# Attention of the first batch by halves of its queries, to start the MLP's first tile earlier

## The chip, the cores and the metric

One core of one Trainium2 chip. The metric is the device time of the whole kernel in microseconds (us), median of several runs. "Ratio" always means: the mean time of one kernel's fast runs over that of the kernel before in the same rounds, so it is not quite the ratio of the medians that are quoted.

## The reference

Softmax attention over 8 batches, 12 heads, 448 positions, head size 64; then a two-layer MLP on the joined heads.

```python
scores = q @ k.T / 8;  attn = softmax(scores);  x = attn @ v      # (8, 12, 448, 64)
x = x.transpose(0, 2, 1, 3).reshape(3584, 768)
h = x @ w_in                                                        # w_in  768 x 2048
out = maximum(0.01 * h, h) @ w_out                                  # w_out 2048 x 768
```

## The kernel before

Heads are taken in pairs: 8 batches x 6 pairs = 48 units. Each unit has eight steps (`slots`). The MLP works on tiles of 384 or 512 token columns; its matmuls ("atoms") are strewn between the steps of later units, so that TensorE always has something to do while ScalarE computes exps. Tile 0 needs the first 384 queries of all six pairs of batch 0, so it cannot start before pair 5 is done. TensorE executes in program order: an MLP matmul that waits holds up the attention behind it.

```python
    def slots(u):                       # eight steps of one pair, shortened
        def s0(): scores(u, 0); scores(u, 1); expo(u, 0)
        def s1(): expo(u, 1); x_transposes(u - 2); dma_transposes(u + 2)
        def s2(): pv(u - 1, 0)
        def s3():
            load(u + 5)                                        # q, k, v of a later pair, SyncE queue
            load_w({2: 1, 3: 2, 4: 2, 5: 2}.get(u, 0))         # weights, GpSimd queue, f32 -> bf16
            transposes(u + 1)                                  # q and k, by TensorE
        def s4(): scores(u, 2); scores(u, 3); expo(u, 2)
        def s5(): expo(u, 3); cast(u + 3)                      # f32 -> bf16 on GpSimd
        def s6(): pv(u - 1, 1)
        ...
    # ... the prologue casts pairs 0 to 2 and issues the first quarter of w_in behind cast(0) ...

    def mlp(i):
        ...
        for m in range(MD):                                    # 16 blocks; a quarter of w_in holds 4
            ps = ps_mm.tile([P, 4 * P], F32, name="mm")        # two PSUM buffers
            for kk in range(KD):                               # 6
                nc.tensor.matmul(ps[:, :n], w_in_sb[:, kk, ts(m, P)], xT[:, kk, at:at + n], ...)
                if kk == KD - 1:
                    nc.scalar.activation(h[:, m, :n], ps[:, :n], AX.Prelu, alpha=0.01)
                yield n
        # ... second product with w_out, 6 results of 16 matmuls of 384 columns ...

    begin = [8 * (HP * (i + 1) + 1) + 7 - 5 * (i == 0) for i in range(B)]   # tile 0 from step 58
    # ... the atoms of tile i are spread evenly over the steps begin[i] to begin[i + 1] ...
```

The softmax here doesn't subtract the row's maximum and nothing guards it: scores larger than these inputs give would overflow.

## Time and profile before

| | before |
|---|---|
| time, median of 4 runs | 427.48 us (426.62 to 428.27) |
| first MLP matmul | 36.16 us |
| first matmul of the second MLP tile (step 111) | 84.50 us |
| span of the profiled run | 425.7 us |

The page cuts the span into 40 slices of 10.6 us; a digit is the busy share of a slice in tenths (for PEclk the granted TensorE clock, for DMA the busy share of the 16 DMA engines).

```profile
PE   6889999999999999999999999999999999999995
...
ACT  4887774467534675466643576456743477214300
...
PEclk8899999999999999999999999999999999999999
DMA  8999999995546765784464977667446450230022
```

TensorE (PE) is full from the fourth slice on. In the second and third slice ScalarE (ACT) is as busy as TensorE, and it sets the pace, as the timelines below show. DMA stays at eight to nine tenths or more for nine slices, to about 95 us: up to about 74 us because the pairs are loaded far ahead and the weights come at the same time.

The timeline of TensorE for one pair in that early stage (start us, length us, engine, line, operation, tile, shapes, count; in brackets the idle time before it and what ended it). L178 are scores, L196 the product with v, L166 and L217 transposes.

```profile
23.82 0.37 PE L217 MATMUL tr<-ident,x 112*128 112x112 bf16 x4
24.03 0.67 PE L196 MATMUL pv<-v,e 112*128 112x65 bf16 x16
24.67 0.55 PE L166 MATMUL tr<-ident,qkb 112*128 112x112 bf16 x8
25.16 0.55 PE L178 MATMUL sc<-qkT 64*128 64x448 bf16 x4
25.64 0.68 PE L196 MATMUL pv<-v,e 112*128 112x65 bf16 x16
26.59 0.36 PE L178 MATMUL sc<-qkT 64*128 64x448 bf16 x2 [0.27 <-DVE rec L203]
27.40 0.36 PE L178 MATMUL sc<-qkT 64*128 64x448 bf16 x2 [0.44 <-ACT e L187]
```

A pair repeats every 3.87 us (the next pair's x transposes start at 27.69 us). ScalarE paces this stage: its four exps of a pair take 3.34 us, with 0.54 us of idle.

```profile
21.75 3.34 ACT L187 ACTIVATE e<-sc 112x896 bf16<-112x896 f32 x4 [0.54 <-PE sc L178]
```

Which waits of TensorE there are before the second tile (waits table, up to 84.5 us: who waited for whom, us in total, times, longest):

```profile
PE sc L178 <- ACT e L187: 3.7, 9, 0.6
PE mm L134 <- DVE warm L131: 1.2, 1, 1.2
PE sc L178 <- DVE rec L203: 1.1, 4, 0.3
```

The start of the MLP and of its second tile, from the timeline of TensorE:

```profile
36.16 0.81 PE L239 MATMUL mm<-xT,w_in_sb 128*128 128x384 bf16 x4
...
84.50 1.03 PE L239 MATMUL mm<-xT,w_in_sb 128*128 128x512 bf16 x3
```

### The profile page before, as it was taken

Reading aid. Unit: us, or ns where it says so; the run is one execution under the profiler, and the core shown is the slowest. Engines: PE = TensorE matmul, PEld = TensorE weight load, DVE = VectorE, ACT = ScalarE, POOL = GpSimd, SP = SyncE. Lnnn points to the kernel's source line nnn. Section 1 sums busy time; section 2 is a strip of 40 time slices with the busy share of each in tenths; the row PEclk is TensorE's granted clock in tenths of the full one; section 3 lists DMA queues with packets and bytes.
Section 4 is the critical chain, followed back from the end, with each engine's and each line's share of the span. In section 5 each row is a group of like instructions: output and inputs, shape, how many; then the busy total and the mean of one; then the engine's idle time right before and its main releaser. Section 6 shows DMA issues by size and latency. Waiting matters only on the chain.

```text
span 425.7 us, 8968 instructions
## 1 busy us (share of the span) xinstructions
PE 411.4 (97%) x3709; PEld 226.3 (53%) x3724; DVE 100.2 (24%) x271; ACT 229.9 (54%) x322; POOL 92.1 (22%) x168
## 2 busy tenths in 40 slices
PE   6889999999999999999999999999999999999995
PEld 2555655544555555544455555554455555654562
DVE  1454323211222212311123212321123211320021
ACT  4887774467534675466643576456743477214300
POOL 5583332422111313112211131221112100000000
PEclk8899999999999999999999999999999999999999
DMA  8999999995546765784464977667446450230022
GB/s 219 257 246 245 249 249 197 256 253 118 125 117 167 209 125 158 187 209 108 104 148 131 183 180 145 177 178 170 117 99 161 99 84 18 56 85 2 0 75 74
DMA packets 98505, 63.66 MB, mean 150 GB/s; under 512 B 55456, under 2 KB 94880, under 8 KB 98464
## 3 DMA queue, kind: packets, MB, share of 16 engines
q1 hardware_dynamic: 90928, 56.56, 55.3%
q0 software_dynamic: 7296, 6.29, 9.4%
q8 instruction: 29, 0.48, 0.5%
q10 hardware_dynamic: 240, 0.23, 0.2%
q14 instruction: 12, 0.10, 0.1%
HBM read 45.61 MB, written 11.01 MB: 133 GB/s over the span
## 4 chain that ended last, share of the span: by engine, by line
PE 83%; DMA 12%; POOL 2%; ACT 1%; issue 1%; DVE 0%; SPq 0%; POOLq 0%
PE mm L256 33%; PE mm L239 31%; PE pv L196 9%; PE sc L178 9%; DMA fv<-in_v_dram 5%; DMA qkT<-qkb 4%; DMA fk<-in_k_dram 2%; DMA xT<-x 1%; ACT e L187 1%; PE tr L166 1%; POOL w_out_sb L124 1%; POOL v L111 1%; POOL w_in_sb L124 0%; POOL qkb L109 0%; POOL qkb L110 0%
## 5 line engine op out<-in xcount | busy, mean ns | idle before, releaser
L187 ACT ACTIVATE e<-sc 112x896 bf16<-112x896 f32 x192 | 167.6, 915 | 107.2 <-PE sc L178 107.2
L239 PE MATMUL mm<-xT,w_in_sb 128*128 128x384 bf16 (+1 forms) x753 | 160.3, 352 | 0.8
L256 PE MATMUL mm<-w_out_sb,h 128*128 128x384 bf16 x896 | 160.2, 326 | 0.0
L256 PEld LDWEIGHTS <-h 128*128 128x128 bf16 x896 | 81.7, 98 | 62.4 <-issue 14.1
L239 PEld LDWEIGHTS <-w_in_sb 128*128 128x128 bf16 x768 | 68.3, 97 | 70.3 <-issue 16.3
L244 ACT ACTIVATE h<-mm 128x384 bf16<-128x384 f32 (+1 forms) x128 | 69.8, 545 | 60.0 <-PE mm L239 59.9
L111 POOL CAST v<-fv 112x512 bf16<-112x512 f32 x48 | 29.6, 617 | 196.1 <-PE pv L196 163.2
L196 PEld LDWEIGHTS <-e 112*128 112x128 bf16 x1536 | 61.4, 98 | 15.6 <-DVE x L204 1.9
L203 DVE RECIPROCAL rec<-pv 112x4 f32<-112x4 f32 x96 | 17.5, 183 | 206.1 <-PE pv L196 205.3
L196 PE MATMUL pv<-v,e 112*128 112x65 bf16 x1536 | 65.3, 194 | 0.1
L178 PE MATMUL sc<-qkT 64*128 64x448 bf16 x384 | 55.4, 360 | 6.0 <-ACT e L187 3.7
L261 DVE COPY o<-mm 128x384 f32<-128x384 f32 x56 | 31.2, 557 | 90.0 <-PE mm L256 89.9
L204 DVE TENSOR_TENSOR x<-pv,rec 112x256 bf16<-112x256 f32 x96 | 40.7, 424 | 3.5 <-DVE rec L203 0.3
L109 POOL CAST qkb<-fq 112x512 bf16<-112x512 f32 x47 | 28.9, 615 | 37.4 <-DMA fq<-in_q_dram 20.6
L178 PEld LDWEIGHTS <-qkT 64*128 64x128 bf16 x384 | 12.1, 94 | 37.7 <-issue 31.3
L110 POOL CAST qkb<-fk 112x512 bf16<-112x512 f32 x47 | 28.9, 614 | 11.8 <-DMA fk<-in_k_dram 11.6
L166 PE MATMUL tr<-ident,qkb 112*128 112x112 bf16 x96 | 7.8, 226 | 1.3 <-POOL qkb L109 0.8
L169 DVE COPY qkT<-tr 128x896 bf16<-128x896 bf16 x12 | 7.4, 620 | 5.4 <-PE tr L166 5.3
L166 PEld LDWEIGHTS <-qkb 112*128 112x128 bf16 x96 | 6.2, 104 | 3.6 <-POOL qkb L109 1.3
L218 DVE COPY xT<-tr 128x448 bf16<-128x448 bf16 x9 | 3.5, 392 | 12.1 <-PE tr L217 12.1
L134 PE MATMUL mm<-warm 128*128 128x512 bf16 x8 | 3.4, 600 | 1.2 <-DVE warm L131 1.2
L124 POOL DMA_DIRECT2D w_out_sb<-in_moe_w_out_dram x4 | 3.5, 877 | 0.0
(17 smaller groups left out, 14.1 us busy)
## 6 DMA issues: line engine op xcount, KB each, us to landing
fq<-in_q_dram SPq DMA_DIRECT2D x48, 224.0 KB, 3.9
fv<-in_v_dram SPq DMA_DIRECT2D x48, 224.0 KB, 4.3
fk<-in_k_dram SPq DMA_DIRECT2D x47, 224.0 KB, 4.1
w_in_sb<-in_moe_w_in_dram POOLq DMA_DIRECT2D x4, 768.0 KB, 15.1
w_out_sb<-in_moe_w_out_dram POOLq DMA_DIRECT2D x4, 768.0 KB, 35.3
out_dram<-o SPq DMA_DIRECT2D x8, 336.0 KB, 3.1
out_dram<-o SPq DMA_DIRECT2D x8, 288.0 KB, 2.7
out_dram<-o SPq DMA_DIRECT2D x8, 240.0 KB, 3.3
```

The lines of the kernel that those rows point to most:

```text
L109: by[0](qk_sb[u][:, 0].rearrange("p so h d -> p h so d"), fq)
L110: by[1](qk_sb[u][:, 1].rearrange("p so h d -> p h so d"), fk)
L111: by[2](v_sb[u % NV][:, :, :, :D], fv)
L166: nc.tensor.transpose(tr[:, i, ts(so, SC)], qk_sb[u][:, i, so], ident[:SC, :SC])
L178: nc.tensor.matmul(ps[:, j, :S], t[j * D:(j + 1) * D, S + c * SC:S + c * SC + P], t[j * D:(j + 1) * D, :S], start=True, stop=True,)
L187: nc.scalar.activation(e[:, :, c, :], sc_t.pop((u, c))[:SC, :, :S], AX.Exp, scale=scale)
L196: nc.tensor.matmul(ps[:, qc, :], e[:, at:at + P], vt[:, j, c, :], start=(c == 0), stop=(c == NSC - 1),)
L204: nc.vector.tensor_mul(x_t[u][:, :, j, :], ps[:SC, :, :D], rec.to_broadcast([SC, NSC, D]))
L239: nc.tensor.matmul(ps[:, :n], w_in_sb[:, kk, ts(m, P)], xT[:, kk, at:at + n], start=(kk == 0), stop=(kk == KD - 1),)
L244: nc.scalar.activation(h[:, m, :n], ps[:, :n], AX.Prelu, alpha=0.01)
L256: nc.tensor.matmul(ps[:, :NW], h[:, m, ts(c, P)], w_out_sb[:, m, ts(w, NW)], start=(m == 0), stop=(m == MD - 1),)
L261: nc.vector.tensor_copy(o[c][:, ts(w, NW)], ps[:, :NW])
```

## The change

Intent: the MLP's first tile starts earlier. For batch 0 each pair is cut into two halves of 224 queries. The first halves of all six pairs run ahead of most second halves, and tile 0's first product runs in two column passes: the first pass (columns 0 to 223) needs only first halves. So it may start after 10 of 12 half-pairs (5.25 pairs' worth of exps) instead of after 7.25 pairs. The weights, loaded as before by the GpSimd queue, are moved behind the cast of pair 5, so that the pairs are not held up by them.

```diff
-    load_w()                                  # prologue, behind cast(0)
+    halves = [(0, 0), (0, 1), (1, 0), (2, 0), (1, 1), (3, 0), (4, 0), (2, 1),
+              (5, 0), (3, 1), (4, 1), (5, 1)]
+    def half_scores(h, cp): ...               # 4 matmuls of 224 columns, one exp of 896
+    def half_pv(h): ...                       # 16 matmuls, one reciprocal, two multiplies
+    def half_x_transposes(h): ...             # 2 transposes, one copy, PSUM tile "tr"
...
+        for lo, hi in ((0, SH), (SH, n)) if i == 0 else ((0, n),):    # SH = 224
+            for m in range(MD): ...           # as before, on columns lo to hi
...
+    half_casts = {1: 3, 3: 4, 5: 5, 8: 6, 10: 7}
+    half_w = {5: 4, 8: 2, 10: 2}
+    half_turns = {1: 1, 2: 2, 4: 3, 5: 4, 7: 5, 11: 6}
+    def half_slots(h):                        # four steps of a half
+        def s0(): half_scores(h, 0)
+        def s1():
+            if h in half_turns: transposes(half_turns[h])      # PSUM tile "tr" too; pool of one
+            if h >= 2: half_x_transposes(h - 2)
+        def s2(): half_scores(h, 1)
+        def s3(): half_pv(h - 1); ...loads, casts, load_w...
...
-    begin = [8 * (HP * (i + 1) + 1) + 7 - 5 * (i == 0) for i in range(B)]
+    begin = [8 * (HP * (i + 1) + 1) + 7 for i in range(B)]
+    begin[0] = 4 * (NH - 2) + 2               # step 42; step 111 stays the start of the second tile
```

More of the change, by code (lines that the diff above doesn't have):

```diff
@@ L52 @@
     r_pool = ctx.enter_context(tc.tile_pool(name="rec", bufs=4))
+    xh_pool = ctx.enter_context(tc.tile_pool(name="xh", bufs=3))
     x_pool = ctx.enter_context(tc.tile_pool(name="x", bufs=3))
@@ L73 @@
     QL = 2 * S
+    SH = S // 2
+    EH = 2 * NSC * SH
     qkT = [qk_pool.tile([P, QL + P - SC], BF16, name=f"qkT{i}") for i in range(NQ)]
@@ L140 @@
         nc.gpsimd.memset(t[:, EL:], 0.0)
+        nc.gpsimd.memset(t[:, EH:EH + P - SC], 0.0)
     for t in qkT:
@@ L218, in x_transposes, with half_scores, half_pv, half_x_transposes @@
         nc.vector.tensor_copy(dst, tr[:, 0, :])
+    halves = [(0, 0), (0, 1), (1, 0), (2, 0), (1, 1), (3, 0), (4, 0), (2, 1),
+              (5, 0), (3, 1), (4, 1), (5, 1)]
+    assert len(halves) == 2 * HP
+    xh_t = {}
+    def half_scores(h, cp):
+        u, ph = halves[h]
+        ps = ps_s.tile([P, 2, 512], F32, name="sc")
+        t = qkT[u % NQ]
+        for i in range(2):
+            c = 2 * cp + i
+            for j in range(2):
+                nc.tensor.matmul(
+                    ps[:, j, ts(i, SH)],
+                    t[j * D:(j + 1) * D, S + c * SC:S + c * SC + P],
+                    t[j * D:(j + 1) * D, ts(ph, SH)],
+                    start=True, stop=True,
+                )
+        e = e_sb[h % NE][:, :EH].rearrange("p (j c s) -> p j c s", j=2, c=NSC)
+        nc.scalar.activation(
+            e[:, :, 2 * cp:2 * cp + 2, :],
+            ps[:SC, :, :S].rearrange("p j (c s) -> p j c s", c=2), AX.Exp, scale=scale,
+        )
+    def half_pv(h):
+        u, _ = halves[h]
+        e, vt = e_sb[h % NE], v_sb[u % NV]
+        ps = ps_pv.tile([P, NSC, D + 1], F32, name="pv")
+        for j in range(2):
+            for qc in range(2):
+                for c in range(NSC):
+                    at = (j * NSC + c) * SH + qc * SC
+                    nc.tensor.matmul(
+                        ps[:, 2 * j + qc, :], e[:, at:at + P], vt[:, j, c, :],
+                        start=(c == 0), stop=(c == NSC - 1),
+                    )
+        x = xh_pool.tile([SC, 2, 2, D], BF16, name="xh")
+        rec = r_pool.tile([SC, NSC, 1], F32, name="rec")
+        nc.vector.reciprocal(rec, ps[:SC, :, D:])
+        for j in range(2):
+            nc.vector.tensor_mul(
+                x[:, :, j, :], ps[:SC, 2 * j:2 * j + 2, :D],
+                rec[:, 2 * j:2 * j + 2].to_broadcast([SC, 2, D]),
+            )
+        xh_t[h] = x
+    ready = {0: 0}
+    def half_x_transposes(h):
+        u, ph = halves[h]
+        x = xh_t.pop(h)
+        tr = ps_tr.tile([P, 2, S], BF16, name="tr")
+        for qc in range(2):
+            nc.tensor.transpose(tr[:, 0, ts(qc, SC)], x[:, qc], ident[:SC, :SC])
+        nc.vector.tensor_copy(xT[:, u, ts(ph, SH)], tr[:, 0, :SH])
+        if u == HP - 1:
+            ready[0] = (ph + 1) * SH
     def store(o, t0):
@@ L235, in mlp @@
         h = h_pool.tile([P, MD, 4 * P], BF16, name="h")
-        for m in range(MD):
-            ps = ps_mm.tile([P, 4 * P], F32, name="mm")
-            for kk in range(KD):
-                nc.tensor.matmul(
-                    ps[:, :n], w_in_sb[:, kk, ts(m, P)], xT[:, kk, at:at + n],
-                    start=(kk == 0), stop=(kk == KD - 1),
-                )
-                if kk == KD - 1:
-                    nc.scalar.activation(h[:, m, :n], ps[:, :n], AX.Prelu, alpha=0.01)
-                yield n
+        for lo, hi in ((0, SH), (SH, n)) if i == 0 else ((0, n),):
+            for m in range(MD):
+                ps = ps_mm.tile([P, 4 * P], F32, name="mm")
+                assert i or hi <= ready[0]
+                for kk in range(KD):
+                    nc.tensor.matmul(
+                        ps[:, :hi - lo], w_in_sb[:, kk, ts(m, P)], xT[:, kk, at + lo:at + hi],
+                        start=(kk == 0), stop=(kk == KD - 1),
+                    )
+                    if kk == KD - 1:
+                        nc.scalar.activation(
+                            h[:, m, lo:hi], ps[:, :hi - lo], AX.Prelu, alpha=0.01
+                        )
+                    yield hi - lo
         todo = [(c, w) for c in range(n // P) for w in range(2)]
@@ L264, in mlp, with s0, s2, s3 @@
                 yield NW
+    loads = {6: (9,), 7: (10, 11), 8: (12, 13)}
+    half_loads = {0: 5, 5: 6, 8: 7, 10: 8}
+    half_casts = {1: 3, 3: 4, 5: 5, 8: 6, 10: 7}
+    half_w = {5: 4, 8: 2, 10: 2}
+    half_turns = {1: 1, 2: 2, 4: 3, 5: 4, 7: 5, 11: 6}
+    def half_slots(h):
+        def s0():
+            half_scores(h, 0)
+        def s1():
+            if h in half_turns:
+                transposes(half_turns[h])
+            if h >= 2:
+                half_x_transposes(h - 2)
+        def s2():
+            half_scores(h, 1)
+        def s3():
+            if h >= 1:
+                half_pv(h - 1)
+            if h in half_loads:
+                load(half_loads[h])
+            if h in half_casts:
+                cast(half_casts[h])
+            load_w(half_w.get(h, 0))
+        return [s0, s1, s2, s3]
+    NH = len(halves)
     def slots(u):
@@ L279, in s1 @@
                 expo(u, 1)
-            if 2 <= u <= NU + 1:
+            if u - HP < 2:
+                half_x_transposes(NH - 2 + u - HP)
+            elif u <= NU + 1:
                 x_transposes(u - 2)
@@ L284, in s2 @@
         def s2():
-            if 1 <= u <= NU:
+            if u == HP:
+                half_pv(NH - 1)
+            elif u <= NU:
                 pv(u - 1, 0)
         def s3():
-            load(u + 5)
-            load_w({2: 1, 3: 2, 4: 2, 5: 2}.get(u, 0))
+            for i in loads.get(u, (u + 5,)):
+                load(i)
             if u + 1 < NU:
@@ L302, in s5 @@
                 expo(u, 3)
+            if u == HP:
+                cast(u + 2)
             cast(u + 3)
         def s6():
-            if 1 <= u <= NU:
+            if HP < u <= NU:
                 pv(u - 1, 1)
@@ L312, in slots @@
         return [s0, s1, s2, s3, s4, s5, s6, s7]
-    steps = [s for u in range(NU + 2) for s in slots(u)]
-    begin = [8 * (HP * (i + 1) + 1) + 7 - 5 * (i == 0) for i in range(B)]
+    steps = [s for h in range(NH) for s in half_slots(h)]
+    steps += [s for u in range(HP, NU + 2) for s in slots(u)]
+    begin = [8 * (HP * (i + 1) + 1) + 7 for i in range(B)]
+    begin[0] = 4 * (NH - 2) + 2
     assert begin[B - 1] == 8 * (NU + 1) + 7
```

## The prediction

> **What bounds the kernel now.** From about 36 us on TensorE: in the table of stretches it is busy 10.00 of every 10 us from 40 to 70, 49.8 to 49.9 of every 50 up to 400. Before 36 us it is ScalarE: four exps take 3.34 us of each 3.87 us pair (timeline), while TensorE needs about 2.6 us for a pair. The MLP, the only filler, starts at 36.2 us; some 17 us of TensorE are lost before it. DMA is full from 1 to 77 us (share 0.9 or more, 247 GB/s).
>
> **What the change does.** The MLP starts at step 42 instead of 58, after 5.25 pairs of exp rather than 7.25. Tile 0 is spread over 69 steps instead of 53. Its first product becomes 96 matmuls of 224 and 96 of 160 columns instead of 96 of 384 (0.163 us each in a run); scaled, 0.095 + 0.07 us, so +0.3 to +1 us of TensorE, and 16 more Prelus. Scores at half width: little. The intent is sound: a half costs two exps, 1.9 us, so by exp alone the MLP could start at 26.5 us, worth about 2 x 1.25 us of TensorE idle.
>
> **What eats it: the weights.** DMA packet records of the trace: pairs alone land one per 2.7 us; with both queues active a w_in quarter takes 6.35 us and a pair 5.8 us, equal bytes each (0.49 MB per 4 us). The Trainium skill, "DMA: Bandwidth & Descriptors", section "Queues, rings and completion order", says the engines round-robin between queues; the trace agrees. From issue on GpSimd to the first packet are another 5.7 us (20.05 to 25.74). Before, quarters were in at 18.5, 32.2, 38.5, 44.9 us, just ahead of the MLP. After, the first weight issue sits behind the cast of pair 5 on GpSimd: pair 5 lands about 19.2, cast until 19.9, first packet about 25.6. Loads of later pairs run ahead, so the queues stay shared. Quarters are usable at about 32.7, 39, 45.5 and 52 us. A pass-1 quarter (24 narrow matmuls, 2.3 us, plus 5 steps of attention at 0.33 us) needs only 4 us, so TensorE, in order, stalls about 6 us at 26.5 and about 2.4 us at each further quarter, attention behind it.
>
> **Sum.** Last quarter 52, plus 2.4 of matmuls and 1.7 of attention: pass 1 (step 62) ends near 56. The other 49 steps: pass 2, 7 + 4.6; second product 15.7 + 11.0: step 111 at about 94.5. Before it was reached at 84.5. From there both are the same and TensorE-bound, so the 10 us are kept, all on the critical path. w_out (7.1 us a quarter) should land at 59 to 81, just in time.
>
> **Predicted:** 437 us, range 431 to 443. Faster by over 2%: 0.03; within 2%: 0.30; slower by over 2%: 0.67.
>
> **What would show it.** First MLP matmul at 32 to 33 us, not 26, TensorE waiting there for w_in (waits table); three more such waits at quarter borders; the clock row dropping near 27 to 35; the second tile's 512-column matmuls beginning near 95 us instead of 84.5.
>
> **What would make it wrong.** Pair loads running dry of buffers while GpSimd is blocked, so quarters take about 4 us: then the stalls mostly vanish and it is 427 to 430. A first packet earlier than 5.7 us after issue: a gain of the same size. Slower: a half clock in the bursts, or DMA transposes of pair 12 late (they cost 0.5 us at 71 already).

## More of the kernel before

The lengths of neighbours overlap in the pipeline; from start to next start, as the chain of waits counts them, sixteen matmuls of `pv` take 0.51 us.

The trace's clock records say: full from 4.20 us, half from 7.61, full again from 14.44 to 424 us.

## The result

| | before | changed |
|---|---|---|
| median of 4 runs | 427.48 us | 440.44 us (439.37 to 440.98) |
| ratio | | 1.030 (95%: 1.0268 to 1.0332) |
| first MLP matmul | 36.16 us | 38.71 us |
| second column pass (step 62) | | 59.51 us |
| second MLP tile (step 111) | 84.50 us | 98.18 us |
| from there to the end | 341.2 us | 341.0 us |
| bytes of 1, 2, 3, 4 w_in quarters moved by, us | 18.5, 32.2, 38.5, 44.9 | 31.1, 37.4, 43.7, 50.1 |
| w_in quarters landed (semaphore), us | 19.2, 33.8, 40.1, 46.4 | 32.0, 38.7, 45.0, 51.6 |

The row of bytes counts all packets of the weights' queue. A quarter can be used only when its semaphore reports the landing, some 0.6 to 1.6 us later in these two traces.

The changed kernel is 3% slower, and the whole loss is made before the second tile starts: 98.18 - 84.50 = 13.7 us; what follows is the same in both. The slices of the changed kernel (11.0 us each):

```profile
PE   7889899999999999999999999999999999999995
...
ACT  4555677566654377446754377546754377304300
...
PEclk9999999999999999999999999999999999999998
DMA  9999999389565676586454677587655540130022
```

ScalarE, which paced the early stage before (8, 8, 7), now is at 5; TensorE is as busy as before. The clock row shows 9 from the start, and it must not be believed here, as the timeline of TensorE shows. L237 are half scores, L257 the product with v, L170 and L278 the transposes:

```profile
21.33 0.56 PE L237 MATMUL sc<-qkT 64*128 64x224 bf16 x4
21.82 0.93 PE L170 MATMUL tr<-ident,qkb 112*128 112x112 bf16 x8
23.47 0.35 PE L278 MATMUL tr<-ident,xh 112*128 112x112 bf16 x2 [0.71 <-DVE qkT L173]
23.75 0.55 PE L237 MATMUL sc<-qkT 64*128 64x224 bf16 x4
24.23 1.06 PE L257 MATMUL pv<-v,e 112*128 112x65 bf16 x16
25.23 0.56 PE L237 MATMUL sc<-qkT 64*128 64x224 bf16 x4
26.09 0.37 PE L278 MATMUL tr<-ident,xh 112*128 112x112 bf16 x2 [0.31 <-DVE xh L265]
```

The same 16 matmuls of `pv` that took 0.67 us in the kernel before take 1.06 us here (0.51 and 0.99 us from start to next start), the same eight transposes 0.93 us for 0.55. TensorE runs at half speed. The trace's first clock record of this run is "full from 43.78 us"; before it there is none, and the row prints 9 for what is not recorded. Two of the four runs list a mean clock of 0.997 and 0.999, the other two 0.961 and 0.958 (over 438 us that is some 34 to 37 us at half speed), and all four are equally long (440.98, 439.37, 440.27, 440.61 us): what differs is whether the slow stretch was recorded. In the trace of experiment 3, which has the same half stage, the records do say half, from 15.00 to 42.30 us (there the gate had opened twice before, from 4.76 and from 11.59 us, and each time shut again after 3.41 us).

So from 6.5 to 38.7 us the chain of waits runs through TensorE and, in each half, through one of two short steps of VectorE (DVE) that it waits for: the copy of the q and k transposes, or the multiply that makes x. The waits table (up to 98.1 us) sums them up:

```profile
PE tr L278 <- DVE qkT L173: 3.6, 5, 0.7
PE tr L278 <- DVE xh L265: 1.6, 5, 0.3
PE mm L304 <- ACT h L309: 1.2, 3, 0.6
```

There is no wait for w_in at all. A half takes 2.65 us, or 3.9 us where q and k are transposed in it, instead of the 1.9 us that two exps cost; ScalarE idles beside it:

```profile
24.40 0.92 ACT L244 ACTIVATE e<-sc 112x896 bf16<-112x896 f32 x1 [1.56 <-PE sc L237]
```

The start of the MLP, the moment at which the clock opens, and the second tile, from the timeline:

```profile
38.71 1.11 PE L304 MATMUL mm<-xT,w_in_sb 128*128 128x224 bf16 x5
...
42.06 1.11 PE L304 MATMUL mm<-xT,w_in_sb 128*128 128x224 bf16 x5
...
44.73 0.64 PE L304 MATMUL mm<-xT,w_in_sb 128*128 128x224 bf16 x5
...
98.18 1.02 PE L304 MATMUL mm<-xT,w_in_sb 128*128 128x512 bf16 x4
```

Five matmuls of 224 columns take 1.11 us up to 43 us and 0.64 us from 44.7 us on. The MLP itself opened the clock.

Why does it stay shut? The Trainium skill, "TensorE: Matmul & The Clock Gate", Part 1 ("What's actually happening"), says that half speed is the default and that a busy window of about 3.4 us opens the gate. The records agree in length: the intervals of the kernel before are 3.41 and 6.83 us. I cut both traces into windows of 3.41 us, counted from the opening, with the table of stretches. In the changed kernel TensorE was busy for 2.50 to 3.11 us of each window between 6.2 and 40.4 us, and the gate stayed shut; the first window with 3.41 us (40.37 to 43.78) opened it. In the kernel before a window with 3.21 us (11.03 to 14.44) did. Once open, it stayed open at 2.70 us. Three rows of the changed kernel's table (stretch, its length, TensorE's busy time, matmuls, then the clock, which reads 1.00 where nothing is recorded, the DMA share and GB/s):

```profile
36.96:40.37 3.41, 3.10 (x33) 1.00 1.18 247
40.37:43.78 3.41, 3.41 (x29) 1.00 1.18 245
43.78:47.20 3.42, 2.70 (x40) 1.00 1.18 245
```

And the row of the kernel before:

```profile
11.02:14.44 3.42, 3.21 (x33) 0.50 1.17 246
```

The theory, then: **the waits of 0.3 and 0.7 us in every half keep the gate shut, and at half speed TensorE paces the stage (clock theory).** The rival is the prediction's: **late weights (weights theory).** The weights arrived nearly when predicted, but the slow stage had pushed the MLP back so far that each quarter was there before it was needed. Whether they would have cost as much with an open clock has to be tried.

### The profile page after: what moved, and what is told of

It reads as the page before. It is cut to its first block, busy times and chain, and to the rows that moved or that the text cites. A ratio compares the mean times of both kernels' runs of the same rounds, so it can differ in the third digit from the quotient of the medians.

```text
span 439.2 us, 9300 instructions
## 1 busy us (share of the span) xinstructions
PE 425.1 (97%) x3868; PEld 239.4 (55%) x3868; DVE 102.6 (23%) x289; ACT 233.5 (53%) x338; POOL 92.1 (21%) x171
## 4 chain that ended last, share of the span: by engine, by line
PE 94%; ACT 2%; DVE 2%; DMA 1%; issue 0%; ACTq 0%
PE mm L323 34%; PE mm L304 34%; PE pv L200 10%; PE sc L182 9%; PE pv L257 2%; PE sc L237 2%; PE tr L170 2%; ACT e L191 1%; DVE qkT L173 1%; DMA fk<-in_k_dram 1%; PE tr L278 1%; DVE xh L265 1%; ACT h L309 0%; DVE rec L263 0%; ACT e L244 0%
## 5 line engine op out<-in xcount | busy, mean ns | idle before, releaser
L191 ACT ACTIVATE e<-sc 112x896 bf16<-112x896 f32 x168 | 148.1, 915 | 99.3 <-PE sc L182 98.7
L304 PE MATMUL mm<-xT,w_in_sb 128*128 128x512 bf16 (+3 forms) x864 | 166.0, 335 | 1.4 <-ACT h L309 1.2
L304 PEld LDWEIGHTS <-w_in_sb 128*128 128x128 bf16 x864 | 75.8, 98 | 70.4 <-issue 19.3
L309 ACT ACTIVATE h<-mm 128x512 bf16<-128x512 f32 (+3 forms) x144 | 72.4, 504 | 62.3 <-PE mm L304 62.3
L200 PEld LDWEIGHTS <-e 112*128 112x128 bf16 x1344 | 54.1, 98 | 12.1
L200 PE MATMUL pv<-v,e 112*128 112x65 bf16 x1344 | 56.8, 194 | 0.0
L182 PE MATMUL sc<-qkT 64*128 64x448 bf16 x336 | 46.4, 355 | 0.0
L208 DVE TENSOR_TENSOR x<-pv,rec 112x256 bf16<-112x256 f32 x84 | 35.7, 425 | 2.9
L244 ACT ACTIVATE e<-sc 112x896 bf16<-112x896 f32 x24 | 21.9, 917 | 15.6 <-PE sc L237 15.6
L182 PEld LDWEIGHTS <-qkT 64*128 64x128 bf16 x336 | 9.6, 94 | 27.3 <-issue 23.7
L237 PE MATMUL sc<-qkT 64*128 64x224 bf16 x96 | 13.0, 374 | 1.4 <-DVE qkT L173 0.7
L257 PEld LDWEIGHTS <-e 112*128 112x128 bf16 x192 | 10.5, 126 | 3.3 <-issue 2.8
L257 PE MATMUL pv<-v,e 112*128 112x65 bf16 x192 | 12.0, 236 | 0.0
L170 PE MATMUL tr<-ident,qkb 112*128 112x112 bf16 x96 | 9.5, 262 | 0.1
```

Of the source, the lines that this page charges most:

```text
L182: nc.tensor.matmul(ps[:, j, :S], t[j * D:(j + 1) * D, S + c * SC:S + c * SC + P], t[j * D:(j + 1) * D, :S], start=True, stop=True,)
L191: nc.scalar.activation(e[:, :, c, :], sc_t.pop((u, c))[:SC, :, :S], AX.Exp, scale=scale)
L200: nc.tensor.matmul(ps[:, qc, :], e[:, at:at + P], vt[:, j, c, :], start=(c == 0), stop=(c == NSC - 1),)
L208: nc.vector.tensor_mul(x_t[u][:, :, j, :], ps[:SC, :, :D], rec.to_broadcast([SC, NSC, D]))
L257: nc.tensor.matmul(ps[:, 2 * j + qc, :], e[:, at:at + P], vt[:, j, c, :], start=(c == 0), stop=(c == NSC - 1),)
L304: nc.tensor.matmul(ps[:, :hi - lo], w_in_sb[:, kk, ts(m, P)], xT[:, kk, at + lo:at + hi], start=(kk == 0), stop=(kk == KD - 1),)
```

## The experiments

All variants start from the changed kernel unless said otherwise. The key moments of each profiled run, in us (the second-last column is the median, before the ratio to the kernel before in the same rounds; a quarter's semaphore comes 0.6 to 2.5 us after the moment in the third column):

| run | first MLP matmul | bytes of 1 to 4 w_in quarters moved by | second pass | second tile | median | ratio (95%) |
|---|---|---|---|---|---|---|
| e1_filler | 33.33 | 32.2, 38.5, 44.9, 51.2 | 57.16 | 96.03 | 438.34 | 1.025 (1.023 to 1.027) |
| e2_order | 35.36 | 33.4, 39.6, 46.0, 52.3 | 59.67 | 98.55 | 439.05 | 1.026 (1.019 to 1.033) |
| e3_early_w | 37.34 | 25.8, 32.1, 38.4, 44.8 | 58.09 | 96.97 | 440.16 | 1.029 (1.028 to 1.031) |
| e4_order_early_w | 29.65 | 27.4, 33.6, 40.1, 46.4 | 53.78 | 92.66 | 434.75 | 1.015 (1.011 to 1.019) |
| e5_filler_order_early_w | 28.73 | 27.0, 33.2, 39.7, 45.9 | 53.41 | 92.16 | 434.15 | 1.014 (1.011 to 1.017) |
| e6_held_loads | 28.58 | 25.2, 29.3, 33.1, 38.0 | 52.08 | 90.96 | 432.69 | 1.010 (1.007 to 1.014) |
| e7_two_passes | 36.85 | 19.3, 33.3, 39.5, 45.9 | 52.97 | 88.42 | 429.61 | 1.004 (1.001 to 1.007) |
| e8_before_filler | 35.55 | 19.1, 31.4, 37.7, 44.1 | | 84.16 | 427.59 | 0.998 (0.995 to 1.001) |
| e9_one_quarter (wrong result) | 29.74 | 28.1, 34.4, 40.8, 47.2 | 47.53 | 87.89 | 429.38 | 1.003 (0.998 to 1.008) |
| e10_held_pair8 | 28.23 | 24.2, 30.3, 34.4, 38.2 | 47.47 | 86.35 | 428.78 | 0.999 (0.992 to 1.006) |

From the second tile to the end of the span every one of these runs took 340.7 to 341.0 us. So the column "second tile" tells the whole story of each. The profiled run of experiment 7 was its slowest (431.22 us, the other five 429.29 to 429.82), so its 88.42 us stands for that run and not for the median.

### 1. Fill the waits

```diff
+    def keep_busy(n):                          # matmuls of 512 columns on a zero tile
+        for _ in range(n):
+            ps = ps_mm.tile([P, 4 * P], F32, name="mm")
+            nc.tensor.matmul(ps, warm[:, :P], warm, start=True, stop=True)
...
         def s1():
             if h in half_turns:
                 transposes(half_turns[h])
+            if 1 <= h <= 9:
+                keep_busy(2 if h <= 4 else 1)
             if h >= 2:
                 half_x_transposes(h - 2)
```

> The changed kernel with idle matmuls (512 columns, on a zero tile) put ahead of the x transposes of half-pairs 1 to 9; nothing else changed, the result stays right. Clock theory (the half-pair stage has a short wait in every half, so the clock gate never opens and TensorE itself becomes the bound there): with the waits filled the clock goes full by about 15 us, a half takes about 2 us, the MLP could start near 27 us. Weights theory (the prediction's, hidden behind the slow clock): it then stops at w_in quarters that land at about 31.5, 38, 44.5 and 51 us, and the total is about 436 us. If the clock is all that is wrong, there is no wait for w_in and the total is about 424 us. If neither: 440 us or more, as the filler only adds work.

The clock opened at 13.56 us and stayed open. TensorE reached the MLP at 32.7 us (later than hoped: of the 3.6 us of waits for the q and k transposes 2.0 were still there, and the waits for x in full, 1.7 us) and then waited for the weights, which it never did in the changed kernel (waits table up to 110 us; the line numbers shift with the edit):

```profile
PE mm L309 <- DMA w_in_sb<-in_moe_w_in_dram: 6.3, 4, 3.1
PE tr L283 <- DVE qkT L173: 2.0, 4, 0.7
```

438.34 us: 2 us gained, not 16. With the early waits filled the clock opened, and it then stayed open although waits of 0.5 and 0.7 us came later; the weights theory holds behind it. The first quarter landed 1.3 us later here than in the changed kernel (33.3 against 32.0 us), so the gain is a little understated.

### 2. Move the waits away instead

```diff
         def s1():
             if h in half_turns:
                 transposes(half_turns[h])
-            if h >= 2:
-                half_x_transposes(h - 2)
         def s2():
             half_scores(h, 1)
+            if h >= 2:
+                half_x_transposes(h - 2)
```

> The changed kernel with one call moved: the x transposes of a half go from before the second scores to after them, so that neither the copy of the qk transposes (0.7 us) nor the x multiply (0.3 us) is waited for. No work added. Clock theory: TensorE has almost no idle in the half stage, the gate opens by about 15 us, as with the filler; then, by the weights theory, waits at the w_in quarters and about 436 us, or 424 us if the weights do not matter. If the slow clock came from the kind of matmul and not from the waits, the clock stays half until the MLP and it is about 438 us.

With no work added, the clock opened at 15.90 us in the profiled run. These are the same matmuls in another order, so their kind alone had not kept it shut. The waits for the two VectorE steps fell from 5.2 to 2.1 us, but did not vanish. TensorE was at the MLP at 28.93 us, and there stood the stall that the prediction had put at 26.5 us, about 6 us long (timeline):

```profile
28.66 0.27 PE L278 MATMUL tr<-ident,xh 112*128 112x112 bf16 x2
35.36 1.11 PE L304 MATMUL mm<-xT,w_in_sb 128*128 128x224 bf16 x5 [6.43 <-DMA w_in_sb<-in_moe_w_in_dram]
```

In this stall the clock shut again (half from 29.55 to 39.79 us), so the first quarter's matmuls ran at half speed; and once more from 53.45 to 56.86 us, at a wait of 3.0 us for the fourth quarter. In this run the v of pair 5 landed 2.3 us later than in the changed kernel (21.17 against 18.87 us), and the weights behind it 3.3 us later (35.3 against 32.0 us): without that the stall would have been about half as long, an estimate from this difference. Whether the delay is chance was not tried. The four runs scatter from 435.17 to 441.43 us; the one whose clock was listed as 1.0 was the 435.17. Against the kernel before the verdict at 2% is unclear (interval 1.019 to 1.033). For the theories it is clear enough, with experiment 1: the open clock alone does not bring the time back.

### 3. Earlier weights alone

```diff
-    half_w = {5: 4, 8: 2, 10: 2}
+    half_w = {1: 1, 3: 1, 5: 2, 8: 2, 10: 2}
```

> The changed kernel with the w_in quarters issued after the casts of pairs 3, 4 and 5 (1, 1, 2 of them) instead of all four after pair 5; about 5 us earlier. Clock theory: weights are not waited for in the changed kernel, so no change: 440 us, within 1.5 us. The prediction's story (late weights cost the 13 us): about 434 us.

All quarters came 5.3 us earlier, and the time stayed (440.16 us). In the changed kernel as it is the weights cost nothing. This is the run that refutes the prediction's story as the story of this kernel.

### 4. Both

The edits of 2 and 3 together.

> Both edits, the moved transposes and the earlier weights. If the clock theory and the weights theory both hold: the clock opens by 15 us, quarters land near 26.5, 33, 39 and 45.5 us, waits for w_in remain but end 5 us earlier than in the run with the moved transposes alone, so about 430 to 431 us, 5 us less than that run. If weights never matter: the same time as that run.

434.75 us: 4.3 us less than with the moved transposes alone, and 5.4 us less than with the early weights alone. Each theory had been tested with the other limit still in place. It stopped 4 us above the expectation: the clock opened only at 17.67 us and shut once more from 48.39 to 51.80 us, behind a wait of 3.1 us for a quarter.

### 5. Filler, moved transposes and early weights

The edits of 1 (filler now in `s2`, ahead of the moved x transposes, and in half 0), 2 and 3 together.

> The changed kernel with filler matmuls, moved x transposes and the earlier weights together. Both theories: clock full from 15 us at the latest and not closed again, MLP from about 27 us, quarters at about 26.5, 33, 39.5 and 46 us, the second column pass from about 51 us, the second tile from about 89.5 us, total about 430 to 431 us. Clock theory alone (no role for the weights): 424 us.

434.15 us, 3 us more than expected. The clock was open from 11.22 us, but TensorE waited for quarters, 5.8 us in four waits, the longest 3.1 us, and the gate shut from 48.76 to 52.18 us. The second pass began at 53.41 us, 5.9 us after the fourth quarter had landed (47.48 us).

### 6. Hold the loads of later pairs

On the kernel of experiment 5. A quarter takes 6.35 us only because SyncE has loads of later pairs in the same engines all the time. Two small copies on the SyncE queue that read a quarter make the loads behind them wait until it has landed.

```diff
-    half_w = {1: 1, 3: 1, 5: 2, 8: 2, 10: 2}
+    half_w = {0: 1, 1: 1, 3: 1, 5: 1, 8: 2, 10: 2}
+    half_gates = {8: 1, 10: 3}                 # ahead of the loads of pairs 7 and 8
+    def hold_loads(i):
+        nc.sync.dma_start(out=hold[:, i // 2],
+                          in_=w_in_sb[:16, 0, i * (DF // 4):i * (DF // 4) + 16])
```

> The previous kernel with the w_in quarters issued earlier still (behind the casts of pairs 2, 3, 4, 5) and the loads of pair 7 held back until the second quarter has landed, those of pair 8 until the fourth (two 512-byte copies on the SyncE queue that read the quarter). Weights theory: with the DMA engines to themselves a quarter takes about 4 us instead of 6.35, quarters near 22, 26, 31 and 36 us, hardly any wait for w_in, the second tile from about 83 to 84 us, total about 424 to 426 us, below the kernel before. If the order of the transfers does not matter, or the held pairs then come too late by as much: no gain, 430 us.

Quarters two and three now took 4.1 and 3.8 us, and no wait for w_in was left. But the 424 to 426 us that the weights theory had promised did not come. Pair 7 came too late (waits table up to 110 us), the clock shut over it (38.95 to 45.78 us), and only 1.5 us were gained:

```profile
PE tr L170 <- POOL qkb L113: 2.1, 1, 2.1
PE tr L170 <- POOL qkb L114: 1.4, 2, 1.1
```

### 7. The two column passes alone, in the kernel before

```diff
-        for m in range(MD):
+        for lo, hi in ((0, S // 2), (S // 2, n)) if i == 0 else ((0, n),):
+            for m in range(MD):
```

> The kernel before with only the two column passes for tile 0's first product, nothing else. It prices that part: 96 matmuls of 224 and 96 of 160 columns for 96 of 384, 16 more Prelus: +1.3 us by the lengths seen in the changed kernel, up to +2.5 us with waits for ScalarE; 428.8 to 430 us. If the passes were the main loss, it would be near 440.

429.61 us; the ratio 1.0038 is 1.6 us (0.5 to 2.8). The passes have a price, but they are not the loss.

### 8. Filler in the kernel before

```diff
     s1:
+            if u <= 2:
+                keep_busy(2 + (u == 0))
     s5:
+            if u <= 2:
+                keep_busy(2)
     transposes(0)
+    keep_busy(3)
```

> The kernel before with filler matmuls in its first three pairs, so that the clock does not close at 7.6 us. Clock theory: the half clock from 7.6 to 14.4 us costs the kernel before only 1 to 2 us, as ScalarE and the loads bound that stretch: 425.5 to 426.5 us. If the clock is worth more there: below 424.

The clock was open from 6.21 us on. 427.59 us, ratio 0.998 with 1 inside the interval: nothing that could be told from noise, and not the 425.5 to 426.5 us expected. In the kernel before the shut gate cost little (at most 2.0 us by the interval, the filler's own cost included), because ScalarE and the loads paced that stretch.

### 9. No waiting for quarters 2 to 4 (wrong result)

```diff
-                        ps[:, :hi - lo], w_in_sb[:, kk, ts(m, P)], xT[...],
+                        ps[:, :hi - lo], w_in_sb[:, kk, ts(m % 4 if i == 0 else m, P)], xT[...],
```

On the kernel of experiment 5: same work, same transfers, but tile 0's first product uses the first quarter only.

> Wrong result on purpose: the kernel with filler, moved transposes and earlier weights, but tile 0's first product takes all its weights from the first quarter of w_in (column block m modulo 4), so that nothing waits for quarters 2 to 4; all transfers and all work stay. It asks what the change would be worth if the weights were never late and the clock open. Weights theory: the 5.6 us of waits at quarters 2 to 4 and the closed clock they bring (48.8 to 52.2 us) go, about 7 us: second tile from about 84.5 to 85.5 us, total 425.5 to 427 us, so level with the kernel before: the 2 pairs of earlier start are eaten by the narrow matmuls. If the change is sound but for the weights: 424 us or less. If the waits for quarters were not the cause of what is left: 434 us as without it.

The waits were gone, the clock stayed open from 13.24 us, and the second pass began at 47.53 us, 5.9 us earlier than in 5. Now TensorE outran the next transfers, w_out (waits table up to 110 us):

```profile
PE mm L309 <- ACT h L315: 1.2, 3, 0.6
PE mm L138 <- DVE warm L135: 1.2, 1, 1.2
PE mm L329 <- DMA w_out_sb<-in_moe_w_out_dram: 1.1, 2, 0.9
```

429.38 us, level with the kernel before (interval 0.998 to 1.008) and 2.4 us above the upper end of what I expected. So even with an open clock and weights that are never late for the first product, the change gains nothing in this form, which still carries the filler of experiment 5.

### 10. Hold only pair 8

On the kernel of experiment 6.

```diff
-    half_gates = {8: 1, 10: 3}
+    half_gates = {10: 2}
```

> The kernel with held loads, now only pair 8 is held, until the third quarter has landed; pair 7 runs free. Pair 7 is then in time, quarters near 25, 31.5, 36 and 42 us, waits of 1 to 3 us at the third and fourth: second tile from about 88 us, 429 us. If the two demands together are more than the DMA engines give in that time, a wait comes back at pair 8 or the quarters and it stays at 431 to 433 us.

The three fast runs took 427.29 to 428.90 us, ratio 0.999 (0.992 to 1.006); a fourth of 434.13 us is left out of the ratio, though not of the median of 428.78. The result is right. One wait of some length is left (pair 8, waits table up to 110 us), and the second tile starts at 86.35 us:

```profile
PE tr L170 <- POOL qkb L114: 1.3, 1, 1.3
PE mm L309 <- ACT h L314: 1.2, 3, 0.6
```

With both limits treated, the halves come back to the kernel before, and not below it. I saw no version that beats both kernels. One rival is untested: this kernel and that of experiment 9 run 14 filler matmuls, and no version had an open clock, weights in time and no filler. An estimate: from its first exp (7.40 us) to the start of the MLP (28.23 us) ScalarE idles for 2.4 us here, which bounds what the filler can cost in that stretch; without it the second tile would begin at 83.9 us at the earliest, against 84.50 us in the kernel before. So without filler a gain of up to 0.6 us is neither shown nor excluded.

## Why the prediction was right, and where it was wrong

**The number was right, the reason was not.** Predicted 437 us (431 to 443), measured 440.44. But the check that the prediction named for itself failed: the first MLP matmul came at 38.71 us, not at 32 to 33, and none of the changed kernel waited for w_in.

- *"A half costs two exps, 1.9 us, so by exp alone the MLP could start at 26.5 us."* This is the step that failed. It took the TensorE times of the kernel before, at full clock, for the new stage. There the gate stayed shut until 43.78 us and a half took 2.65 to 3.9 us; the MLP started at 38.71 us. The prediction listed a half clock only for "the bursts", after the weights. The shut gate is shown by matmul lengths, and that short waits caused it is shown by experiments 1 and 2, which filled or moved the waits and opened it by 13.6 and 15.9 us (one profiled run each; experiments 4 and 5 agree, with 17.67 and 11.22 us).
- *"TensorE, in order, stalls about 6 us at 26.5."* Not in this kernel (experiment 3: weights 5.3 us earlier, no change). It is true one layer down: with the clock open the stall was there, 6.43 us (experiment 2).
- *Weight arrival.* Predicted usable at 32.7, 39, 45.5 and 52 us; landed at 32.0, 38.7, 45.0 and 51.6 us, 6.3 to 6.7 us apart. The equal sharing of the DMA engines and the 5.7 us from issue to first packet held (issue 19.55, first packet 25.14 us).
- *The sum.* Pass 1 ends at 56: measured 59.5 us. The other 49 steps: 38.3 us predicted, 38.7 measured. Step 111: 94.5 predicted, 98.18 measured. After it "both are the same": 341.2 and 341.0 us. That the total came near is luck: two limits of like size cover the same stretch. The slow stage ends the first pass at 59.5 us, and with the clock open the late weights end it at 57.2 us (experiment 1; 59.7 us in experiment 2, where the stalls shut the clock again and the weights came later).
- *The narrow matmuls* were put at +0.3 to +1 us; the passes alone cost 1.6 us (0.5 to 2.8), with waits for ScalarE in it (1.2 us in the changed kernel).
- *"The intent is sound ... worth about 2 x 1.25 us."* Experiment 9 took away late w_in quarters with the clock open and came out level with the kernel before. That the passes, the waits for ScalarE (1.2 us) and the filler take what the earlier start gives is argued; they were not separated.

How the 13.7 us split cannot be said by adding two numbers, as the limits overlap. By the start of the second tile: opening the clock alone gave 2.2 us (experiment 1) or nothing (experiment 2, whose stall shut it again), early weights alone 1.2 us in the profiled run and nothing in the medians (experiment 3), both 5.5 to 6 us (4 and 5), both and a better order of transfers 11.8 us (10). The rest, 86.35 against 84.50 us, has the size of what the passes cost in experiment 7 (1.6 us); that it is the same cost is argued, not shown.

What stays open: how much activity exactly opens the gate. In the runs here every window of 3.41 us with TensorE busy throughout opened it, but windows of 93% and 97% in experiments 4 and 2 did not, and single ones of 83% to 96% did. Leaving the transposes out of the count sorts them no better: a busy window with 1.43 us of transposes opened it in experiment 3 (8.17 to 11.58 us), one with 0.37 us (busy 3.10 us) did not in the changed kernel (33.54 to 36.96 us). The windows were counted from the opening, and TensorE's busy time in them does not decide alone.

## What to carry to other kernels

Read the clock from the lengths of equal matmuls, not only from the clock row, and ask of a finer-grained schedule whether its new short waits keep TensorE at half speed. When a change starts a consumer earlier, work out when its data can be there at all with the transfers that share the engines: here both limits cost nearly the same, each hid the other, and removing one alone showed almost nothing. An experiment that removes a suspected cost and finds no gain refutes it only as the first limit; try it again with the other limit removed.

## What the Trainium skill lacked or had wrong

- "TensorE: Matmul & The Clock Gate", Part 1, does not say how busy a window must be to open the gate, and its advice under "Why this matters for your kernels" (no idle gaps over about 3 us) speaks of gaps that shut it; what it says of shorter idles between groups of matmuls gives no size. Here gaps of 0.31 and 0.71 us, in windows up to 91% busy, went with a shut gate in every window from 6.2 to 40.4 us, while an open gate stayed open at 79% busy.
- The same page warns that clock events in a trace can be unreliable. The first event of the changed kernel's profile is at 43.78 us; what lies before it is missing, and the clock row printed 9 for a stretch in which 16 `pv` matmuls took 0.99 us instead of 0.51 us.
- "DMA: Bandwidth & Descriptors", "Specifications", gives about 1 us to the first byte for transfers issued by GpSimd. The casting loads of w_in (768 KB each after the cast) took 5.6 to 5.8 us from issue to the first packet in the two kernels (19.55 to 25.14; 20.05 to 25.74; 6.19 to 12.04 us) and 5.1 to 6.3 us in experiments 2 and 6 (21.85 to 26.92; 12.40 to 18.74 us), with the SyncE queue busy all the while.
- The same page, "Queues, rings and completion order", says that engines round-robin between queues, and that was borne out in bytes: 0.50 and 0.47 MB from the two queues in 4 us (after the cast), 6.3 us for a quarter when shared, and 3.8 to 4.1 us when the other queue was held (experiment 6). It says that transfers from all issuing engines share the DMA engines and interleave, but gives no figure for what loads running ahead on one queue cost the urgent ones on the other: here 2.2 to 2.5 us a quarter.
